# Decayed attention and two feed-forward layers on one core: the block quad's products in another order, low parts of sums on GpSimd, the high part of g and the low part of weights one step later

## The chip, the cores and the metric

One core of one Trainium2 chip. The kernel is one launch; the metric is the device time of that launch in microseconds (us), the median of repeated runs. All numbers are float32 at the interface.

## The reference

The reference computes a causal attention with decay and puts its output through two feed-forward layers:

```python
# attention, per batch (2) and head (8), 768 positions in blocks, head size 64
intra = ((q_b @ k_b.T) * Dmask) @ v_b            # Dmask[i, j] = lam ** (i - j), i >= j
inter = (q_b * lam ** (pos + 1)) @ kv_state
out_b = intra + inter
kv_state = lam ** block * kv_state + (k_b * lam ** (block - 1 - pos)).T @ v_b
...
x = out.reshape(1536, 512)                       # 1536 tokens, 512 features
h = x @ w_in1;  g = h * clip(h + 3, 0, 6) / 6;  x = g @ w_out1     # d_ff = 2048
h = x @ w_in2;  g = maximum(h, 0) ** 2;         out = g @ w_out2
```

The weights of the layers arrive as float64, the rest as float32.

## The kernel before

**Split numbers.** TensorE multiplies in a float32 format of fewer bits (F32R). Every operand is therefore held as a high part (the number rounded to F32R, made by a cast on ScalarE) and a low part (the number less its high part, made on VectorE), and a product is three matmuls: high by high, high by low, low by high. A matmul here has a 128x128 stationary operand and a 128x512 moving one.

**Weights.** A tile of weights (512 KB of float64) is loaded by SyncE into one of three raw buffers and decoded by ScalarE and VectorE in five pieces, `decode_steps` (L155): `shift` (ScalarE L168 and VectorE L169; it also asks ScalarE for the magnitude of the next tile, L149), `join` (VectorE L174, and the cast to the high part, ScalarE L177), `clamp` of the next tile (L153), `add` (VectorE L181), `rest` (VectorE L184: the low part). A decoded tile takes a slot: five for input weights (`wi`), six for output weights (`wo`). There are 16 `wi` and 16 `wo` tiles to a layer, 64 in all.

**Layers.** The 1536 tokens are three blocks j = 0, 1, 2 of 512. The 2048 hidden features are 16 tiles f, in groups g of four. For each group the hidden products h are made, g is computed from them in `gate` (L450: for the first layer ScalarE L457, VectorE L459, ScalarE cast L463, VectorE low part L465; for the second ScalarE L461, L462, L463, VectorE L465), and `project` (L584) adds the group's contribution to the four output tiles of a block: `y(j, g)` is four units of 12 matmuls, each followed by an addition to `acc` on VectorE (L606) or, in the first group, a copy on ScalarE (L603).

**The quad.** In groups 1 to 3, blocks 0 and 1 by a pair of feature tiles (p = f // 2) form a 2x2 block product that `seven` (L498) makes of seven block products of six matmuls instead of eight, with sums of weights (`weight_sums`, GpSimd L204, four differences into `Ts`; split by `weight_sums_split` L214 into `Th` on ScalarE L222 and `Tl` on VectorE L224) and sums of tokens (`token_sums`, GpSimd L482; split in L494 and L496). `seven` is a generator: each `yield` ends a step. Its seven steps need, in the order of the code before: the first weight tile; `Th`, `Tl` number 3; number 2; the first tile's second half; number 1; number 4; the second tile. Copies between PSUM banks (ScalarE L529, L535, L539) and two additions (VectorE L545, L548) tie them together. `Th` and `Tl` have one buffer, so the next pair's split must follow the last use of this pair's.

**What sets the order.** All engines but SyncE run in the order of the code (`manual_schedule`). The units of TensorE's work stand in a hand-written list, `units` (L667): `q` is a step of a quad, `y` an output tile, `h` a block of hidden products outside the quads, `t` a `weight_sums_split`. Between them a planner with fixed costs (`UNIT` 2.72, `ONE` 0.44, `TWO` 0.7, `FOUR` 1.24, `SCALAR` 0.8) keeps two clocks, `pe_t` and `dve_t`: `vector` (L255) and `unit` (L260) call `decode_until` (L247), which puts decode pieces into VectorE's and ScalarE's queues as long as `dve_t` lies behind. `weight` (L266) forces the pieces of a tile that is needed and not decoded. A `wo` tile's slot comes free after the last unit of `y(2, g)`, which stands in group g + 1; of the four `wo` tiles of a group two fit into slots ahead and two, called the later ones below, must wait for that.

Of the kernel before, what the change touches and what calls it, by code (L numbers as in the profile page):

```python
# [17 lines left out]
P = 128  # L18
# [15 lines left out]
def decay_attention_moe_moe(  # L34
# [120 lines left out]
    def decode_steps(n):  # L155
# [16 lines left out]
        def join():  # L172

            nc.vector.scalar_tensor_tensor(  # L174
                u, t[:, :, 1], -(2**31), u, op0=ALU.bitwise_and, op1=ALU.bitwise_or
            )
            nc.scalar.copy(hi, u.bitcast(F32))  # L177

        def add():

            nc.vector.tensor_tensor(up, u, up, op=ALU.add)  # L181

# [6 lines left out]
        steps = [(ONE, shift), (TWO, join), (ONE, lambda: clamp(n + 1)), (TWO, add), (TWO, rest)]  # L189
        if kind == "wi" and f >= GROUP:  # L190
            full_t[layer, f] = up.bitcast(F32)
            if f % 2:
                steps.append((0.01, lambda: weight_sums(layer, f // 2)))
        return steps

# [15 lines left out]
    def sums_free():  # L211
        return not t_sum and keys[n_begun - 1][1] in s_done

    def weight_sums_split(layer, p):  # L214
# [8 lines left out]
        vector(dve_t + 2 * SCALAR, FOUR)  # L223
        nc.vector.tensor_tensor(lo, t, hi.bitcast(F32), op=ALU.subtract)  # L224
        t_t[layer, p] = (hi, lo)

    def decode_piece():
        nonlocal n_begun
        if not pieces:
            if n_begun == len(keys):  # L230
                return 0
            if not w_free[keys[n_begun][0]]:
                return 0
            pieces.extend(decode_steps(n_begun))
            n_begun += 1
# [46 lines left out]
    ident = const.tile([P, P], F32, name="ident")  # L282
# [77 lines left out]
    def state_values(c):  # L360
# [13 lines left out]
        if not last:  # L374
# [7 lines left out]
            else:  # L382
                kvs = ap.tile([P, NP, D], F32, tag="kvs", name="kvs", bufs=1)
# [66 lines left out]
    def gate(layer, j, f, ph):  # L450
# [34 lines left out]
    def token_sums_split(layer, n):  # L485
# [9 lines left out]
        vector(dve_t + 2 * SCALAR, FOUR)  # L495
        nc.vector.scalar_tensor_tensor(lo, t, scale, hi.bitcast(F32), op0=ALU.mult, op1=ALU.subtract)  # L496
# [5 lines left out]
    def seven(layer, p):  # L502
# [26 lines left out]
        nc.scalar.copy(b, a)  # L529
        yield  # L530
# [237 lines left out]
```

## Time and profile before

| | us |
|---|---|
| median of 3 runs (650.87 to 652.54) | 652.13 |
| the profiled execution | 651.67 |
| its span, first to last instruction | 649.9 |
| TensorE busy in it | 583.5 |
| VectorE busy | 414.5 |
| ScalarE busy | 327.4 |
| GpSimd busy | 96.4 |

"Busy" is the union of an engine's instruction times. Matmuls overlap each other, so that 90% busy is not 90% of the peak; what TensorE lost is read from how many matmuls lie in a stretch. "Idle before" of an instruction is the time in which its engine did nothing in front of it, with the instruction that ended the wait behind the arrow. PEclk is the clock that TensorE was granted: 1.00 is 2.4 GHz, 0.50 is 1.2 GHz.

### The profile page before, as it was taken

Reading aid. Unit: us, or ns where it says so; the run is one execution under the profiler, and the core shown is the slowest. Engines: PE = TensorE matmul, PEld = TensorE weight load, DVE = VectorE, ACT = ScalarE, POOL = GpSimd, SP = SyncE. Lnnn points to the kernel's source line nnn. Section 1 sums busy time; section 2 is a strip of 40 time slices with the busy share of each in tenths; the row PEclk is TensorE's granted clock in tenths of the full one; section 3 lists DMA queues with packets and bytes.
Section 4 is the critical chain, followed back from the end, with each engine's and each line's share of the span. In section 5 each row is a group of like instructions: output and inputs, shape, how many; then the busy total and the mean of one; then the engine's idle time right before and its main releaser. Section 6 shows DMA issues by size and latency. Waiting matters only on the chain. (4 is left out here: it accounts for less than half of the span.)

```text
span 649.9 us, 7777 instructions
## 1 busy us (share of the span) xinstructions
PE 583.5 (90%) x2950; PEld 464.2 (71%) x2950; DVE 414.5 (64%) x639; ACT 327.4 (50%) x545; POOL 96.4 (15%) x92
## 2 busy tenths in 40 slices
PE   8899989986999869988799989987899869989797
PEld 5677767865787648866588878776688648877586
DVE  6799986636974489555998763634982369433422
ACT  2344666545443365344654874758454485256120
POOL 3785102200210002100021012200210002100000
PEclk9899999999899979999799999999799979999699
DMA  9952220300420024000331210400420024000012
GB/s 327 406 212 89 72 98 32 98 0 27 136 98 0 2 86 140 32 1 0 130 98 33 88 42 0 131 0 7 155 97 1 1 74 153 1 0 1 32 66 97
DMA packets 18037, 49.79 MB, mean 77 GB/s; under 512 B 2128, under 2 KB 2128, under 8 KB 18000
## 3 DMA queue, kind: packets, MB, share of 16 engines
q1 hardware_dynamic: 17856, 49.04, 21.6%
q8 instruction: 23, 0.38, 0.2%
q10 hardware_dynamic: 144, 0.26, 0.2%
q14 instruction: 14, 0.11, 0.1%
HBM read 46.14 MB, written 3.15 MB: 76 GB/s over the span
## 5 line engine op out<-in xcount | busy, mean ns | idle before, releaser
L606 DVE TENSOR_TENSOR acc<-acc,py 128x512 f32<-128x512 f32 x72 | 49.1, 682 | 51.9 <-PE py L568 51.6
L441 PE MATMUL ph<-xh,wih 128*128 128x512 f32 x192 | 75.1, 391 | 3.1 <-DVE g L459 3.1
L441 PE MATMUL ph<-xh,wil 128*128 128x512 f32 x192 | 74.7, 389 | 0.0
L441 PE MATMUL ph<-xl,wih 128*128 128x512 f32 x192 | 74.7, 389 | 0.0
L204 POOL TENSOR_TENSOR Ts<-dt 128x256 f32<-128x256 f32 x24 | 20.8, 886 | 330.2 <-DVE dt L181 203.2
L181 DVE CUSTOM_DVE_ANT_0 dt<-da,dt 128x1024 uint16<-128x1024 uint16 x64 | 48.6, 759 | 0.1
L174 DVE SCALAR_TENSOR_TENSOR da<-raw,da 128x512 int32<-128x512 int32 x64 | 47.3, 739 | 1.7
L149 ACT ACTIVATE da<-raw 128x512 f32<-128x512 f32 x64 | 42.5, 664 | 3.8 <-DVE dt L181 3.4
L441 PEld LDWEIGHTS ph<-xh,wih 128*128 128x128 f32 x192 | 36.0, 188 | 11.5 <-DVE g L459 4.0
L168 ACT ACTIVATE dt<-raw 128x512 int32<-128x512 uint32 x64 | 42.9, 670 | 0.0
L441 PEld LDWEIGHTS ph<-xh,wil 128*128 128x128 f32 x192 | 36.0, 188 | 7.6
L441 PEld LDWEIGHTS ph<-xl,wih 128*128 128x128 f32 x192 | 36.0, 188 | 7.4
L153 DVE TENSOR_SCALAR da<-da 128x512 f32<-128x512 f32 x64 | 32.5, 509 | 13.3 <-ACT da L149 13.0
L568 PE MATMUL py<-woh,gA 128*128 128x512 f32 x80 | 32.0, 414 | 4.7 <-ACT woh L177 4.7
L169 DVE TENSOR_SCALAR da<-da 128x512 int32<-128x512 int32 x64 | 36.0, 562 | 0.0
L177 ACT CAST woh<-da 128x512 fp32r<-128x512 f32 x32 | 19.7, 616 | 29.3 <-DVE da L174 29.1
L459 DVE SCALAR_TENSOR_TENSOR g<-g,ph 128x512 f32<-128x512 f32 x24 | 16.4, 684 | 27.5 <-ACT g L457 27.5
L462 ACT ACTIVATE g<-g 128x512 f32<-128x512 f32 x48 | 30.4, 632 | 1.5
L517 PE MATMUL pq<-S,Th 128*128 128x512 f32 x96 | 29.9, 392 | 1.1 <-ACT pq L529 1.0
L177 ACT CAST wih<-da 128x512 fp32r<-128x512 f32 x32 | 19.8, 618 | 20.0 <-DVE da L174 19.8
L465 DVE TENSOR_TENSOR gA<-g,gA 128x512 fp32r<-128x512 f32 x19 | 13.3, 700 | 25.0 <-ACT gA L463 24.9
L457 ACT ACTIVATE g<-pq,three 128x512 f32<-128x512 f32 x24 | 16.4, 685 | 23.0 <-PE pq L517 23.0
(159 smaller groups left out, 1453.4 us busy)
## 6 DMA issues: line engine op xcount, KB each, us to landing
raw<-in_w_in SPq DMA_DIRECT2D x32, 512.0 KB, 3.2
raw<-in_w_out SPq DMA_DIRECT2D x32, 512.0 KB, 3.3
out<-acc SPq DMA_DIRECT2D x12, 256.0 KB, 2.0
kT<-in_kT SPq DMA_DIRECT2D x6, 256.0 KB, 5.5
k<-in_k SPq DMA_DIRECT2D x6, 256.0 KB, 5.6
v<-in_v SPq DMA_DIRECT2D x6, 256.0 KB, 5.0
lentS<-in_kT SPq DMA_DIRECT2D x6, 256.0 KB, 5.2
lentS<-in_qT SPq DMA_DIRECT2D x6, 256.0 KB, 5.4
```

Of the source, the lines that this page charges most:

```text
L149: nc.scalar.activation(abs_t[n], raw_t[n][:, :, 1].bitcast(F32), AF.Abs, scale=2.0**16)
L153: nc.vector.tensor_scalar(abs_t[n], abs_t[n], 2.0, (1.875 - 2.0**-23) * 2.0**32, op0=ALU.max, op1=ALU.min)
L168: nc.scalar.activation(up, t[:, :, 0].bitcast(U32), AF.Copy, scale=2.0**-29)
L169: nc.vector.tensor_scalar(u, u, 3, None, op0=ALU.logical_shift_left)
L174: nc.vector.scalar_tensor_tensor(u, t[:, :, 1], -(2**31), u, op0=ALU.bitwise_and, op1=ALU.bitwise_or)
L177: nc.scalar.copy(hi, u.bitcast(F32))
L181: nc.vector.tensor_tensor(up, u, up, op=ALU.add)
L441: nc.tensor.matmul(ph, w[:, a * P : (a + 1) * P], x[:, a, :], start=a == 0 and i == 0, stop=a == KD - 1 and i == 2,)
L462: nc.scalar.activation(g, g, AF.Square)
L517: nc.tensor.matmul(ps, u, v, start=start and a == 0 and i == 0, stop=a == KH - 1 and i == 2, skip_group_check=True)
L568: nc.tensor.matmul(py, a, b, start=f == fs[0] and i == 0, stop=f == fs[-1] and i == 2)
L606: nc.vector.tensor_tensor(t, t, py, op=ALU.add)
```

## The change

It reorders the steps of a quad (the first tile's second half becomes step 2) and the units of groups 1 to 3 (the four units of `y(2, g - 1)` come earlier); it makes the high part of a decoded weight in `add`, from the joined number as before, and its low part in the next tile's pieces; in the first layer it makes the high and low part of g at the next call of `settle`; it takes the products with the low part of g last in an output tile; it moves the low parts of weight sums, and of the first layer's token sums, from VectorE to GpSimd; and it gives a third buffer to g, paid for by letting `ident` and `kvs` share the buffers `Th` and `Ts`.

```diff
         def join():
...
-            nc.scalar.copy(hi, u.bitcast(F32))
-
         def add():
             nc.vector.tensor_tensor(up, u, up, op=ALU.add)
+            nc.scalar.copy(hi, u.bitcast(F32))
+            rests.append((TWO, rest))
+            if kind == "wi" and f >= GROUP and f % 2:
+                rests.append((0.01, lambda: weight_sums(layer, f // 2)))
...
-        steps = [(ONE, shift), (TWO, join), (ONE, lambda: clamp(n + 1)), (TWO, add), (TWO, rest)]
         if kind == "wi" and f >= GROUP:
             full_t[layer, f] = up.bitcast(F32)
-            if f % 2:
-                steps.append((0.01, lambda: weight_sums(layer, f // 2)))
+        steps = [(ONE, shift), (TWO, join), (ONE, lambda: clamp(n + 1)), (TWO, add)]
+        steps[1:1] = rests
+        rests.clear()
         return steps
...
     def sums_free():
-        return not t_sum and keys[n_begun - 1][1] in s_done
+        return not t_sum and min(full_t)[0] in s_done
...
         nc.scalar.copy(hi, t)
-        vector(dve_t + 2 * SCALAR, FOUR)
-        nc.vector.tensor_tensor(lo, t, hi.bitcast(F32), op=ALU.subtract)
+        nc.gpsimd.tensor_tensor(lo, t, hi.bitcast(F32), op=ALU.subtract)
...
-    ident = const.tile([P, P], F32, name="ident")
+    ident = wsp.tile([P, 2 * DM], F32, tag="Th", name="ident")[:, :P]
...
-                kvs = ap.tile([P, NP, D], F32, tag="kvs", name="kvs", bufs=1)
+                kvs = wsp.tile([P, KD, DM // 2], F32, tag="Ts", name="kvs")[:, :, :D]
...
-        g = gp.tile([P, n], F32, tag="g", name="g")
+        g = gp.tile([P, n], F32, tag="g", name="g", bufs=3)
+        g_t[layer, j, f] = (gh, gl, s)
         if layer == 0:
             nc.scalar.activation(g, ph, AF.Relu, bias=three)
             vector(pe_t + SCALAR, TWO)
             nc.vector.scalar_tensor_tensor(g, g, 6.0, ph, op0=ALU.min, op1=ALU.mult)
+            settle()
+            unsplit.append((g, gh, gl))
         else:
             nc.scalar.activation(g, ph, AF.Relu)
             nc.scalar.activation(g, g, AF.Square)
-        nc.scalar.copy(gh, g)
-        vector(dve_t + SCALAR if layer == 0 else pe_t + 3 * SCALAR, TWO)
-        nc.vector.tensor_tensor(gl, g, gh.bitcast(F32), op=ALU.subtract)
-        g_t[layer, j, f] = (gh, gl, s)
+            unsplit.append((g, gh, gl))
+            settle(pe_t + 2 * SCALAR)
+
+    def settle(ready=0.0):
+        for g, gh, gl in unsplit:
+            nc.scalar.copy(gh, g)
+            vector(max(dve_t, ready) + SCALAR, TWO)
+            nc.vector.tensor_tensor(gl, g, gh.bitcast(F32), op=ALU.subtract)
+        unsplit.clear()
...
-        vector(dve_t + 2 * SCALAR, FOUR)
-        nc.vector.scalar_tensor_tensor(lo, t, scale, hi.bitcast(F32), op0=ALU.mult, op1=ALU.subtract)
+        if layer == 0:
+            nc.gpsimd.tensor_tensor(lo, t, hi.bitcast(F32), op=ALU.subtract)
+        else:
+            vector(dve_t + 2 * SCALAR, FOUR)
+            nc.vector.scalar_tensor_tensor(lo, t, scale, hi.bitcast(F32), op0=ALU.mult, op1=ALU.subtract)
...
         nc.scalar.copy(b, a)
+        settle()
+        yield
+        prod(a, wi(f0, 1), x(0, k2), False)
+        gate(layer, 0, f0, a)
         yield
...
         nc.scalar.copy(s7, e)
+        settle()
         yield
         prod(b, tw(2), s(2), False)
         c = bank()
         nc.scalar.copy(c, b)
+        vector(pe_t + SCALAR, TWO)
+        nc.vector.tensor_tensor(b, b, s7, op=ALU.add)
         yield
-        prod(a, wi(f0, 1), x(0, k2), False)
-        gate(layer, 0, f0, a)
-        yield
-        vector(dve_t, TWO)
-        nc.vector.tensor_tensor(b, b, s7, op=ALU.add)
         prod(c, tw(1), s(1), False)
...
-    def products(layer, j, grp, e, f, py):
+    def products(layer, j, grp, e, f, py, part=range(3)):
...
+        prods = ((woh, gh), (wol, gh), (woh, gl))
+        for i in part:
...
-            for f in fs:
-                products(layer, j, grp, e, f, py)
+            for part in ((0, 1), (2,)):
+                for f in fs:
+                    products(layer, j, grp, e, f, py, part)
...
-            units += q(p) * 3 + y2[:1] + q(p) * 2 + y2[1:2] + q(p) * 2 + [("t", l, p + 1)] + y2[2:3]
+            units += q(p) + y2[:1] + q(p) * 3 + y2[1:2] + q(p) * 2 + [("t", l, p + 1)] + y2[2:3] + q(p)
             p += 1
-            units += q(p) * 3 + h(2, f0) + q(p) * 2 + y2[3:] + q(p) * 2 + h(2, f1)
+            units += q(p) + y2[3:] + q(p) * 3 + h(2, f0) + q(p) * 2 + h(2, f1) + q(p)
             units += y(l, 1, g) + h(2, f2) + h(2, f3)
```

`settle()` is also called at the start of `project` and `project_by_unit`, and `decode_piece` emits waiting `rests` when no tile can be begun.

The first place where this shows is VectorE's queue in the second layer's group 2, from the addition of the last unit of `y(2, 1)` (L606 before, L628 now, into `acc_3363` and `acc_3341`) to the first of the two later `wo` tiles. Before:

```order
L606 TENSOR_TENSOR acc_3363<-acc_3363,py 128x512
L465 TENSOR_TENSOR gA<-g,gA 128x512 x2
L465 TENSOR_TENSOR gq<-g,gv 128x512
L169 TENSOR_SCALAR da<-da 128x512
L174 SCALAR_TENSOR_TENSOR da<-raw,da 128x512
L153 TENSOR_SCALAR da<-da 128x512
L181 ISA dt<-da,dt 128x1024
L184 TENSOR_TENSOR wol_924<-dt,woh_923 128x512
```

Now (L565 and L569 are the quad's additions L545 and L548, L481 is the low part of g, L180 and L187 are L181 and L184):

```order
L628 TENSOR_TENSOR acc_3341<-acc_3341,py 128x512
L481 TENSOR_TENSOR gq<-g,gv 128x512
L565 TENSOR_TENSOR pq<-pq,s_3982 128x512
L169 TENSOR_SCALAR da<-da 128x512
L174 SCALAR_TENSOR_TENSOR da<-raw,da 128x512
L153 TENSOR_SCALAR da<-da 128x512
L180 ISA dt<-da,dt 128x1024
L169 TENSOR_SCALAR da<-da 128x512
L187 TENSOR_TENSOR wol_899<-dt,woh_898 128x512
L174 SCALAR_TENSOR_TENSOR da<-raw,da 128x512
L481 TENSOR_TENSOR gdecay<-g,gdecay 128x512
L569 TENSOR_TENSOR pq_3975<-pq,s_3982 128x512
```

The decoding of the later tiles stood behind all gates of the second pair's steps and its addition L548; now it stands behind step 4's addition L565 and ahead of L569, and the low part L187 has the next tile's shift in front of it.

The second place is ScalarE's queue in the first layer's group 2, at the last gates before `y(1, 2)` and the casts of the two later `wo` tiles. Before:

```order
L457 ACTIVATE g<-pq,three 128x512
L463 CAST gkv<-g 128x512
L457 ACTIVATE g<-ph,three 128x512
L463 CAST gh_805<-g 128x512
L168 ACTIVATE dt<-raw 128x512
L149 ACTIVATE da<-raw 128x512
L177 CAST woh_1183<-da 128x512
L168 ACTIVATE dt<-raw 128x512
L149 ACTIVATE da<-raw 128x512
L177 CAST woh_1201<-da 128x512
```

Now (L464 is L457, L479 is L463, L181 is L177; `pq_1950` holds the second tile of block 1):

```order
L464 ACTIVATE g<-pq,three 128x512
L479 CAST gv<-g 128x512
L181 CAST woh_1190<-da 128x512
L464 ACTIVATE g<-pq_1950,three 128x512
L479 CAST gdecay<-g 128x512
L168 ACTIVATE dt<-raw 128x512
L149 ACTIVATE da<-raw 128x512
L464 ACTIVATE g<-ph,three 128x512
L479 CAST gh_834<-g 128x512
L464 ACTIVATE g<-pq,three 128x512
L479 CAST gkv<-g 128x512
```

Before, each gate's cast followed its own activation and both later tiles came behind the last gate. Now a cast follows the next gate's activation, and the tiles' pieces stand between the gates: the cast into `gh_834`, of the value in `pq_1950`, has a cast of the previous value, two pieces of a weight and another gate's activation in front of it.

The third place is GpSimd's queue at the start of the first layer's quads. Before:

```order
L482 TENSOR_TENSOR s_779<-xf_197,s_777 128x1024
L482 TENSOR_TENSOR s_940<-xf_197,xf_435 128x1024
L204 TENSOR_TENSOR Ts<-dt 128x256 x2
L204 TENSOR_TENSOR Ts<-dt,Ts 128x256 x2
L204 TENSOR_TENSOR Ts<-dt 128x256 x2
```

Now (L498 is L482, L512 the low part of token sums, L209 is L204, L228 the low part of weight sums):

```order
L498 TENSOR_TENSOR s_779<-xf_197,s_777 128x1024
L512 TENSOR_TENSOR S_930<-s_775,S_930 128x1024
L498 TENSOR_TENSOR s_933<-xf_197,xf_434 128x1024
L512 TENSOR_TENSOR S_1009<-s_777,S_1009 128x1024
L512 TENSOR_TENSOR S_1101<-s_779,S_1101 128x1024
L512 TENSOR_TENSOR xl_424<-s_933,xh_423 128x1024
L209 TENSOR_TENSOR Ts<-dt 128x256 x2
L209 TENSOR_TENSOR Ts<-dt,Ts 128x256 x2
L228 TENSOR_TENSOR Tl<-Ts,Th 128x1024
L209 TENSOR_TENSOR Ts<-dt 128x256 x2
```

Four low parts of token sums have joined it ahead of the first weight sums, and one low part follows each set of weight sums.

## Rows read from the trace of the kernel before

**Rows 1.** The page: busy time, and TensorE's granted clock in 40 slices.
```profile
PE 583.5 (90%) x2950; PEld 464.2 (71%) x2950; DVE 414.5 (64%) x639; ACT 327.4 (50%) x545; POOL 96.4 (15%) x92
...
PEclk9899999999899979999799999999799979999699
```

**Rows 2.** Waits of TensorE: engine, line, releaser, us in total, times, longest.
```profile
PE py L568 <- ACT woh L177: 29.3, 12, 4.3
PE pq L517 <- ACT Th L222: 8.4, 6, 1.7
PE py L568 <- DVE wol L184: 5.0, 9, 1.0
PE pq L517 <- DVE Tl L224: 3.2, 6, 0.5
```

**Rows 3.** The chain in order of time, a stretch without waits: start, us, what.
```profile
549.70 10.88 PE py L568 x48
```

**Rows 4.** Stretches round waits at y(1, g): us, PE busy, PEclk, DMA, GB/s.
```profile
155.00:170.00 15.00, 9.15 (x26) 0.77 0.33 105
449.00:464.00 15.00, 9.15 (x27) 0.77 0.31 106
598.00:613.50 15.50, 10.24 (x27) 0.67 0.04 17
```

**Rows 5.** The same view round waits for Th and Tl.
```profile
136.00:141.00 5.00, 2.92 (x11) 1.00 0.00 0
579.00:583.00 4.00, 2.34 (x9) 1.00 0.00 0
```

**Rows 6.** Timeline of ScalarE, first layer, group 2: start, us, instruction.
```profile
232.44 0.68 ACT L457 ACTIVATE g<-ph,three 128x512 f32<-128x512 f32 x1
233.89 0.62 ACT L463 CAST gh<-g 128x512 fp32r<-128x512 f32 x1 [0.77 <-DVE g L459]
234.41 0.67 ACT L168 ACTIVATE dt<-raw 128x512 int32<-128x512 uint32 x1
234.98 0.65 ACT L149 ACTIVATE da<-raw 128x512 f32<-128x512 f32 x1
235.54 0.60 ACT L177 CAST woh<-da 128x512 fp32r<-128x512 f32 x1
236.05 0.66 ACT L168 ACTIVATE dt<-raw 128x512 int32<-128x512 uint32 x1
```

**Rows 7.** The same view of VectorE, the later tiles' decoding.
```profile
237.41 0.42 DVE L169 TENSOR_SCALAR da<-da 128x512 int32<-128x512 int32 x1
237.86 0.69 DVE L174 SCALAR_TENSOR_TENSOR da<-raw,da 128x512 int32<-128x512 int32 x1
238.47 0.42 DVE L153 TENSOR_SCALAR da<-da 128x512 f32<-128x512 f32 x1
238.81 0.68 DVE L181 CUSTOM_DVE_ANT_0 dt<-da,dt 128x1024 uint16<-128x1024 uint16 x1
239.60 0.69 DVE L184 TENSOR_TENSOR wol<-dt,woh 128x512 fp32r<-128x512 f32 x1
240.21 0.42 DVE L169 TENSOR_SCALAR da<-da 128x512 int32<-128x512 int32 x1
```

**Rows 8.** Groups of instructions by line: VectorE's low parts of sums, ScalarE's Th.
```profile
L224 DVE TENSOR_TENSOR Tl<-Ts,Th 128x1024 fp32r<-128x1024 f32 x12 | 14.7, 1222 | 1.5 <-ACT Th L222 1.5
...
L222 ACT CAST Th<-Ts 128x1024 fp32r<-128x1024 f32 x12 | 12.5, 1046 | 4.7 <-POOL Ts L204 4.7
```

**Rows 9.** Timeline of GpSimd and VectorE at one token sum.
```profile
345.66 2.71 POOL L482 TENSOR_TENSOR s<-acc,s 128x1024 f32<-128x1024 f32 x1 [4.04 <-DVE acc L606]
346.03 2.62 DVE L153 TENSOR_SCALAR da<-da 128x512 f32<-128x512 f32 x1
...
348.57 0.68 DVE L614 SCALAR_TENSOR_TENSOR xl<-acc,xh 128x512 fp32r<-128x512 f32 x1
```

**Rows 10.** Timeline of TensorE: the first hidden product, and waits in the first groups.
```profile
55.65 0.50 PE L441 MATMUL ph<-xh,wih 128*128 128x512 f32 x1
...
78.92 0.50 PE L441 MATMUL ph<-xh,wih 128*128 128x512 f32 x1 [1.22 <-DVE g L459]
...
83.84 0.50 PE L441 MATMUL ph<-xh,wih 128*128 128x512 f32 x1 [1.90 <-DVE g L459]
...
383.97 0.50 PE L568 MATMUL py<-woh,gv 128*128 128x512 f32 x1 [1.69 <-ACT gv L463]
...
645.73 0.39 PE L568 MATMUL py<-woh,gkv 128*128 128x512 f32 x1
```

More of the change, by code (lines that the diff above doesn't have):

```diff
@@ L187, in rest @@
             load_ahead(n + 1 + RAW)
-        steps = [(ONE, shift), (TWO, join), (ONE, lambda: clamp(n + 1)), (TWO, add), (TWO, rest)]
         if kind == "wi" and f >= GROUP:
             full_t[layer, f] = up.bitcast(F32)
-            if f % 2:
-                steps.append((0.01, lambda: weight_sums(layer, f // 2)))
+        steps = [(ONE, shift), (TWO, join), (ONE, lambda: clamp(n + 1)), (TWO, add)]
+        steps[1:1] = rests
+        rests.clear()
         return steps
+    rests = []
     full_t, t_sum, t_t, s_done = {}, {}, {}, set()
@@ L229, in decode_piece @@
         if not pieces:
[L230 to L235, printed above, removed]
+            if n_begun < len(keys) and w_free[keys[n_begun][0]]:
+                pieces.extend(decode_steps(n_begun))
+                n_begun += 1
+            else:
+                pieces.extend(rests)
+                rests.clear()
+        if not pieces:
+            return 0
         if pieces[0][0] < ONE and not sums_free():
@@ L462, in gate @@
             nc.scalar.activation(g, g, AF.Square)
-        nc.scalar.copy(gh, g)
-        vector(dve_t + SCALAR if layer == 0 else pe_t + 3 * SCALAR, TWO)
-        nc.vector.tensor_tensor(gl, g, gh.bitcast(F32), op=ALU.subtract)
-        g_t[layer, j, f] = (gh, gl, s)
+            unsplit.append((g, gh, gl))
+            settle(pe_t + 2 * SCALAR)
+    unsplit = []
+    def settle(ready=0.0):
[4 more added lines that the diff above has]
+        unsplit.clear()
     s_sum, s_t = {}, {}
@@ L494, in token_sums_split @@
         nc.scalar.activation(hi, t, AF.Copy, scale=scale)
-        vector(dve_t + 2 * SCALAR, FOUR)
-        nc.vector.scalar_tensor_tensor(lo, t, scale, hi.bitcast(F32), op0=ALU.mult, op1=ALU.subtract)
+        if layer == 0:
+            nc.gpsimd.tensor_tensor(lo, t, hi.bitcast(F32), op=ALU.subtract)
+        else:
+            vector(dve_t + 2 * SCALAR, FOUR)
+            nc.vector.scalar_tensor_tensor(lo, t, scale, hi.bitcast(F32), op0=ALU.mult, op1=ALU.subtract)
         if n == 1:
@@ L556, in seven @@
         gate(layer, 0, f1, c)
-    def products(layer, j, grp, e, f, py):
+    def products(layer, j, grp, e, f, py, part=range(3)):
         es = slice(e * P, (e + 1) * P)
-        fs = range(GROUP * grp, GROUP * (grp + 1))
         gh, gl, _ = g_t[layer, j, f]
         woh, wol = weight(("wo", layer, f))
-        if layer == 0:
-            prods = ((woh[:, es], gh), (woh[:, es], gl), (wol[:, es], gh))
-        else:
-            prods = ((gh[:, es], woh), (gh[:, es], wol), (gl[:, es], woh))
-        for i, (a, b) in enumerate(prods):
-            nc.tensor.matmul(py, a, b, start=f == fs[0] and i == 0, stop=f == fs[-1] and i == 2)
+        prods = ((woh, gh), (wol, gh), (woh, gl))
+        for i in part:
+            w, g = prods[i]
+            a, b = (w[:, es], g) if layer == 0 else (g[:, es], w)
+            nc.tensor.matmul(py, a, b, start=f % GROUP == 0 and i == 0, stop=f % GROUP == GROUP - 1 and i == 2)
     def project_by_unit(layer, j, grp, f):
         n = BLOCKS[j] * P
+        settle()
         free_weights()
@@ L588, in project @@
         fs = range(GROUP * grp, GROUP * (grp + 1))
+        settle()
         if py is None:
```

## The prediction

> **What bounds the kernel now.** I read the page first: TensorE is busy 90% of the span, VectorE 64%, ScalarE 50%, GpSimd 15%, and TensorE's granted clock dips to 0.7 and below at regular distances [rows 1]. So TensorE is the bound, and the dips ask what it waits for.
>
> The chain's stretches without waits give the price of its work: 48 matmuls in 10.88 us, 0.2267 us each [rows 3]. By the code the layers have 576 (L441), 504 (L517) and 1152 (L568) of them: 2232, or 506.0 us. The first starts at 55.65 and the last ends at 646.12 [rows 10], 590.5 us. TensorE thus loses 84.5 us, in idle time and at the lower clock.
>
> The waits name the places [rows 2]: y(1, g) waits for the two later `wo` tiles (29.3 + 5.0 us), quads for `Th` and `Tl` (8.4 + 3.2). What such a place costs in all, clock included, is read from stretches around it. A matmul is shown for 0.39 us but follows its neighbour at 0.2267, so at the edges 1.7 more are counted than fit, and the loss is length - (count - 1.7) x 0.2267. At y(1, g) that is 9.5, 9.3 and 9.8 us [rows 4]; there are six such places (groups 1 to 3, two layers): **57 us**. The clock of these stretches is 0.77 to 0.67: after the waits TensorE runs matmuls at 1.2 GHz for some us. Round `Th` and `Tl` it is 2.9 in the first layer and 2.4 in the second, at a clock of 1.00 [rows 5]; six places, 11.6 us by the waits alone, 15.9 by these two: **15 us**. The other 12 us lie in the layers' first groups and at small waits.
>
> **The change, part by part.**
>
> *Order of units.* Before, 2 steps and one h stand between the end of y(2, g - 1), which frees the slots, and y(1, g): 2 x 1.36 + 2.72 = 5.4 us. Now 6 steps and two h do: 13.6 us. The decoding begins in VectorE's queue behind step 4's addition L565, 1.4 us into the last 9.5 us of those. I walk ScalarE's and VectorE's queues from the end of step 4 (t = 0), with the distances from start to start that the timelines show [rows 6, 7] (ScalarE 0.52 to 0.57, and 0.65 where one needs the other; VectorE 0.60, 0.34 for L153, 0.45 for L169, 0.80 from L181 to L184). y(1, g) starts at 9.5, and its first two tiles take four matmuls (0.9 us) now that the low parts of g come last.
>
> First layer: first later tile decoded at 5.7, second at 11.0; needed at 10.4 and 11.1. So the weights are in time, by little. The value in `pq_1950` is not: its activation is behind the cast of a weight that waits for L180 at 7.9, and its cast stands behind two weight pieces and the activation of h(2, f1) (the second order shown above); it ends at 11.8, wanted at 10.9: 0.9 us. Its low part is ready at 13.7, wanted at 13.0: 0.8 us. A wait costs about 0.3 more than its idle time (at `Th` and `Tl` 15 for 11.6 in twelve waits), so two of them make **2.2 us** a group, 6.6 for three.
>
> Second layer: three ScalarE instructions to a gate but only one of VectorE. The tiles are ready at 6.0 and 10.5, the high part of the fourth tile's g at 11.3, wanted at 10.9: **0.7 us** a group, 2.1 for three.
>
> *What the walk hides.* Eight tiles a group are now decoded between step 4 and the group's end, about 37 us: 8 x 2.8 us (from one L169 to the next [rows 7]) + 9 additions and 14 gate pieces of 0.6 = 36 us of VectorE in the first layer. It just fits. Should it not, what is late next is L628's additions, which hold PSUM banks; three banks give 5 us of slack, so I take nothing.
>
> *Th and Tl.* They now have 9.5 us of TensorE's work (y, step 7, step 1, y, step 2) between the end of step 6 and their first use, where they had 4.1. ScalarE needs two gates and 1.05 for `Th` [rows 8], about 5 in all; `Tl` on GpSimd is not in the trace, but the nearest row, a token sum of the same shape and engine, has 2.71 [rows 9]. Lowest bound 1.22, VectorE's own [rows 8]; highest 2.71 plus one VectorE instruction of 0.7 in front. I take 2.7: 5 + 2.7 = 7.7 < 9.5. All **15 us** go, with 2 us to spare.
>
> *Low parts on GpSimd.* Sixteen instructions of 1.22 leave VectorE. In return each can hold it: L153 took 2.62 instead of 0.42 while a token sum ran, and ended 0.3 us after it [rows 9]. At worst that is 16 x (2.6 - 1.2) = 22 us of VectorE, at best a gain of 20. In the quads VectorE has nothing but gate parts with TensorE's slack before them; I take nothing there.
>
> The Trainium skill (GPSIMD Engine Reference, Engine selection) says to leave elementwise work on VectorE, GpSimd being about twice as slow. The rows agree on the size (2.71 against 1.22), and by that rule alone this part would be a loss: with all 22 us on TensorE's path the sum below would be 610.
>
> *First groups.* In the first layer the late cast takes a wait out of ScalarE's chain (0.77 us a gate [rows 6]), but three GpSimd instructions hold VectorE among the gates, and a fourth delays the first `Ts`, for which a decode activation then waits in ScalarE's queue ahead of four output copies. I walk it to 3 us lost before y(0, 0) and 3 at y(1, 0), where 6.2 were lost: nothing gained. In the second layer gh of the last tile stays late (1.69 before [rows 10]; I get 2.5), and the small waits behind it go: -1.5.
>
> *At no cost:* the third g buffer, the shared `ident` and `kvs` (each is dead before the next user writes; attention's GpSimd chain is as long), `rest` one piece later (0.45 us, with `wi` tiles decoded 10 us ahead). Loads move with `rest`: SyncE asks for a raw tile 0.45 us later, against three buffers.
>
> **The sum,** against the profiled execution: 651.7 - 57 - 15 + 6.6 + 2.1 - 1.5 = 586.9; I add 1 for waits of a few tenths that no walk finds: 588. The median of the runs is 0.5 above the profiled one, so **588.3**.
>
> **The rivals.**
>
> 1. *The walk is short at y(1, g).* If VectorE comes one hold (2.6 us) late there, TensorE waits about 5 us instead of 2.2, and the clock falls as it does now. Price: a stretch loses 9.5 [rows 4], of which 5.7 is idle ((29.3 + 5.0) / 6 [rows 2]), so the clock and restarts take 3.8; (2.6 + 3.8) x 6 = 38, **626**. For it: the first layer's margins are tenths. Against it: `Tl` is over 4 us before y(2, g - 1) ends, so no hold lies in that stretch, and the waits of about 2 us for `Th` and `Tl` leave the clock at 1.00 [rows 5].
>
> 2. *Slower: GpSimd's hold sets VectorE's pace.* Each of sixteen low parts would hold a gate long enough that TensorE waits 2.6 us and loses 3.8 at the lower clock: 16 x 6.4 = 102, 588 + 102 = **690**. It decides from the point at which TensorE's slack behind the held instruction is under 2.6 us. Against it: in the quads that slack is a whole y (2.72) or more at every gate, and the hold of [rows 9] falls into a slice (the 22nd) whose clock is 0.9 or more [rows 1]. The rule of the Trainium skill named above (GPSIMD Engine Reference, Engine selection) points this way.
>
> 3. *The change does not do what it says.* The planner's clocks put the later tiles' pieces so far back that y(1, g) forces them as before; then only `Th` and `Tl` go: **637**. The order shows them ahead, so this needs a wait at run time that the queue's order does not show, as for a slot or a raw tile.
>
> 4. *Better:* no wait at y(1, g) at all and half of the first groups' losses gone: 652.1 - 72 - 5 = **575** to 580.
>
> **How the numbers follow.** Forecast 0.68 (580 to 600), better 0.10, rival 1 0.12, rival 3 0.05, rival 2 0.03, no change 0.02. The range takes in the better case's nearer half, 577; above, a wait of one hold at each y(1, g) without the clock's fall, 588 + 16 = 604, and the 2 us of `Tl`'s spare: 606. Left out are rivals 1 to 3, 2 in 10. About 0.3% (2 us) is what a measurement can tell: faster 0.95, within it 0.02, slower 0.03.
>
> **What would show it.** Right: the waits for L181 (the cast of `wo`) and for `Th` are gone from TensorE's list; what stands there is L479's cast, one to two us a place, three in the first layer larger than three in the second; PEclk is 1.00 in the middle of every group; `Tl` L228 on GpSimd takes 2.4 to 2.9; VectorE instructions of over 2 us beside it. Wrong: PEclk still dips once a group (rival 1), TensorE waits on VectorE right behind L228 (rival 2), or L181 leads the list (rival 3).

## The result, and the profile after

| | us | ratio to the kernel before, 95% interval |
|---|---|---|
| before, in the same session | 651.64 | |
| changed kernel | 578.32 (577.75 to 579.11) | 0.8875 [0.8857, 0.8893] |
| forecast | 588.3 (577 to 606) | |
| profiled execution | 577.75, span 576.0 | |

The kernel is 73 us faster, 10 us more than forecast. The time is inside the range, 1.3 us above its lower end; it lies among the times of rival 4 (575 to 580), which had a chance of 0.10, and not among the forecast's own (580 to 600). The page of the changed kernel, the lines that answer to [rows 1]:

```profile
PE 555.6 (96%) x2950; PEld 456.8 (79%) x2950; DVE 407.8 (71%) x623; ACT 323.4 (56%) x545; POOL 143.4 (25%) x108
...
PEclk9999999999999999999999999999999999999999
```

The same 2950 matmuls are busy for 28 us less, because in the layers they no longer run at a lower clock: every slice of PEclk is 0.9 or more, where each group had one of 0.8, 0.7 or 0.6. GpSimd has 47 us more. The waits of TensorE (engine, line, releaser, us in total, times, longest), all of 0.5 us or more:

```profile
PE psc L361 <- DVE A L362: 6.4, 6, 2.5
PE py L587 <- ACT gh L479: 2.1, 1, 2.1
PE py L587 <- ACT acc L625: 1.7, 1, 1.7
PE warm L661 <- DVE idle L295: 1.5, 1, 1.5
PE py L587 <- DVE gkv L481: 1.3, 2, 0.7
PE pq L536 <- ACT pq L548: 0.9, 1, 0.9
PE pxt L402 <- DVE A L362: 0.8, 1, 0.8
PE py L587 <- DVE gq L481: 0.7, 1, 0.7
PE py L587 <- DVE gl L481: 0.7, 1, 0.7
```

All four waits of [rows 2] are gone: TensorE has no wait in this list for the casts of `wo` (now L181), for its low parts (L187), for `Th` (L227) or `Tl` (L228). psc, warm and pxt belong to the attention ahead of the layers, which the change leaves alone but for the shared buffers. Two stretches round y(1, 1), first and second layer, as in [rows 4]:

```profile
147.00:162.00 15.00, 14.27 (x63) 1.00 0.30 102
402.00:417.00 15.00, 15.00 (x68) 1.00 0.31 106
```

63 matmuls stand where 26 stood, at a clock of 1.00. By the prediction's formula the first loses 15 - 61.3 x 0.2267 = 1.1 us and the second nothing, where 9.5 and 9.3 were lost. And the two ends of the layers:

```profile
56.10 0.50 PE L447 MATMUL ph<-xh,wih 128*128 128x512 f32 x1
...
571.80 0.39 PE L587 MATMUL py<-woh,gA 128*128 128x512 f32 x1
```

The layers take 516.1 us for 506.0 us of matmuls. TensorE loses **10 us** there, where it lost 84.5; the difference, 74 us, is that of the two spans (649.9 and 576.0).

### The profile page after: what moved, and what is told of

Its sections match the earlier page's. It is cut to its first block, busy times and chain, and to the rows that moved or that the text cites. A ratio compares the mean times of both kernels' runs of the same rounds, so it can differ in the third digit from the quotient of the medians.

```text
span 576.0 us, 7778 instructions
## 1 busy us (share of the span) xinstructions
PE 555.6 (96%) x2950; PEld 456.8 (79%) x2950; DVE 407.8 (71%) x623; ACT 323.4 (56%) x545; POOL 143.4 (25%) x108
## 4 chain that ended last, share of the span: by engine, by line
PE 73%; DVE 13%; ACT 5%; issue 4%; DMA 2%; SPq 1%; POOL 1%; DVEq 0%
PE py L587 39%; PE pq L536 19%; PE ph L447 14%; DVE dt L180 2%; DVE da L153 1%; DVE da L174 1%; DVE g L466 1%; DMA lentS<-in_qT 1%; DVE xl L419 1%; DVE A L362 1%; DMA lentS<-in_k 1%; DVE wol L187 1%; ACT da L149 1%; DVE da L169 1%; POOL Ts L209 1%
## 5 line engine op out<-in xcount | busy, mean ns | idle before, releaser
L628 DVE TENSOR_TENSOR acc<-acc,py 128x512 f32<-128x512 f32 x72 | 48.7, 683 | 34.6 <-PE py L587 34.5
L209 POOL TENSOR_TENSOR Ts<-dt 128x256 f32<-128x256 f32 x24 | 22.6, 963 | 160.7 <-DVE dt L180 136.6
L228 POOL TENSOR_TENSOR Tl<-Ts,Th 128x1024 fp32r<-128x1024 f32 x12 | 29.9, 2492 | 103.3 <-ACT Th L227 81.9
L180 DVE CUSTOM_DVE_ANT_0 dt<-da,dt 128x1024 uint16<-128x1024 uint16 x64 | 50.7, 792 | 0.0
L174 DVE SCALAR_TENSOR_TENSOR da<-raw,da 128x512 int32<-128x512 int32 x64 | 48.0, 750 | 0.3
L153 DVE TENSOR_SCALAR da<-da 128x512 f32<-128x512 f32 x64 | 35.5, 555 | 2.9 <-ACT da L149 2.9
L169 DVE TENSOR_SCALAR da<-da 128x512 int32<-128x512 int32 x64 | 36.8, 575 | 0.0
L481 DVE TENSOR_TENSOR gq<-g,gv 128x512 fp32r<-128x512 f32 x20 | 16.0, 801 | 25.6 <-ACT gv L479 25.5
L181 ACT CAST wih<-da 128x512 fp32r<-128x512 f32 x32 | 19.9, 620 | 19.3 <-DVE da L174 19.3
L464 ACT ACTIVATE g<-pq,three 128x512 f32<-128x512 f32 x24 | 16.2, 690 | 25.4 <-PE pq L536 24.9
L587 PE MATMUL py<-woh,gA 128*128 128x512 f32 x80 | 29.8, 389 | 0.0
L187 DVE TENSOR_TENSOR wol<-dt,woh 128x512 fp32r<-128x512 f32 x32 | 23.8, 742 | 7.5 <-ACT woh L181 7.5
```

What stands on the lines that cost most here:

```text
L153: nc.vector.tensor_scalar(abs_t[n], abs_t[n], 2.0, (1.875 - 2.0**-23) * 2.0**32, op0=ALU.max, op1=ALU.min)
L169: nc.vector.tensor_scalar(u, u, 3, None, op0=ALU.logical_shift_left)
L174: nc.vector.scalar_tensor_tensor(u, t[:, :, 1], -(2**31), u, op0=ALU.bitwise_and, op1=ALU.bitwise_or)
L228: nc.gpsimd.tensor_tensor(lo, t, hi.bitcast(F32), op=ALU.subtract)
L587: nc.tensor.matmul(py, a, b, start=f % GROUP == 0 and i == 0, stop=f % GROUP == GROUP - 1 and i == 2)
L628: nc.vector.tensor_tensor(t, t, py, op=ALU.add)
```

## The experiments

Theory A is the prediction's: the order of steps and units makes the gain. Theory B: the relief of VectorE and ScalarE (low parts on GpSimd, later casts, low parts of g last) makes it, and the order only goes with it. Theory C, within A: a good part of the price was the clock that fell behind the idle time. "Loss" below is start-to-start time of TensorE beyond 0.2267 us a matmul, "late" a wait of TensorE for the thing named. Unless another base is named, an edit is made to the changed kernel.

**The order alone.** The kernel before with the new order of steps and units:

```diff
         nc.scalar.copy(b, a)
         yield
+        prod(a, wi(f0, 1), x(0, k2), False)
+        gate(layer, 0, f0, a)
+        yield
...
-            units += q(p) * 3 + y2[:1] + q(p) * 2 + y2[1:2] + q(p) * 2 + [("t", l, p + 1)] + y2[2:3]
+            units += q(p) + y2[:1] + q(p) * 3 + y2[1:2] + q(p) * 2 + [("t", l, p + 1)] + y2[2:3] + q(p)
             p += 1
-            units += q(p) * 3 + h(2, f0) + q(p) * 2 + y2[3:] + q(p) * 2 + h(2, f1)
+            units += q(p) + y2[3:] + q(p) * 3 + h(2, f0) + q(p) * 2 + h(2, f1) + q(p)
```

> The kernel before with the new order of the quad's seven steps and of the units alone; every cast, low part and sum stays where it was before. Theory A (the order makes the gain): the wo slots come free 13.6 us of TensorE's work ahead of y(1, g) instead of 5.4, and t stands 9.5 us ahead of its use instead of 4.1, so nearly all of 57 + 15 us goes; a low part or a high part of g that is a few tenths to 2 us late stays at each of the six y(1, g): 582 to 598 us, L181 and L222 gone from TensorE's waits. Theory B (the relief of VectorE and ScalarE makes the gain, the order only goes with it): the tiles still come late, 610 us or more, the granted clock still dips once a group. Theory C (much of the price was the clock that follows the idle time, 3.8 of 9.5 us a place): as A, and the granted clock is 0.99 or more although waits of 1 to 2 us stay.

Measured: 588.61 us, ratio 0.9027 [0.9004, 0.905]. Of the gain of 73 us, 63 come from the order alone; theory B's 610 or more is out. Waits of TensorE for the steps and the layers:

```profile
PE ph L441 <- DVE g L459: 3.1, 2, 1.9
PE py L568 <- ACT gh L463: 3.0, 2, 2.8
...
PE py L568 <- DVE wol L184: 1.4, 2, 0.7
```

L177 (29.3 us before) and L222 (8.4) are gone from the list. The first line is that of the first group, unchanged from before [rows 10]; the third shows that two tiles are still late, by 0.7 us each.

**All but the order.** The changed kernel with the two `units` lines and the steps of the quad as they were.

> The changed kernel with the old order of the quad's steps and of the units; low parts on GpSimd, the later high part of g, the later low part of the weights and the products with the low part of g at the end stay. Theory A: 5.4 us of TensorE's work between the free slots and y(1, g) cannot hide two decodings, the 57 us stay but for a few us, and Tl on GpSimd (2.5 us instead of 1.22) makes the waits at Th and Tl longer, 15 to 25 us: 640 to 662 us, the clock dips once a group. Theory B: the relief shortens the decoding enough, 595 to 620 us.

Measured: 644.84 us, ratio 0.9881 [0.9861, 0.9901]. Theory A, within its range. Its waits:

```profile
PE py L587 <- ACT woh L181: 22.6, 12, 4.1
PE py L587 <- DVE wol L187: 10.4, 12, 1.7
PE pq L536 <- POOL Tl L228: 7.5, 6, 1.7
...
PE pq L536 <- ACT Th L227: 3.4, 3, 1.1
```

At y(1, g) TensorE is idle for 33.0 us, against 34.3 before: the relief only moves the wait from the cast to the low part. `Tl` on GpSimd, used 4.1 us after t stands, is waited for longer than on VectorE (7.5 against 3.2 in [rows 2]), but `Th`, which is waited for first, for less (3.4 against 8.4); the two together take 10.9 us against 11.6. By layers they differ: a place costs 0.8 us of idle time in the first, where it cost 2.2, and 2.8 in the second, where it cost 1.7. Whether the move of `Tl` alone is a loss in the old order is not shown, as no run makes it without the other edits.

**The low parts back on VectorE.**

```diff
-        nc.gpsimd.tensor_tensor(lo, t, hi.bitcast(F32), op=ALU.subtract)
+        vector(dve_t + 2 * SCALAR, FOUR)
+        nc.vector.tensor_tensor(lo, t, hi.bitcast(F32), op=ALU.subtract)
         t_t[layer, p] = (hi, lo)
```

and, for the first layer's tokens, the line on VectorE of the kernel before.

> The changed kernel with the low parts of the sums (twelve Tl, four of tokens) back on VectorE. Theory A: VectorE gets 16 x 1.22 = 20 us of work back and loses the holds beside GpSimd; in the quads it has slack either way: 576 to 582 us, within 1% of the changed kernel. Theory B: the relief is needed, VectorE's queue is full over the group (36 us of 37), so 1.22 us a quad comes on top of waits at y(1, g) and the PSUM banks: 12 x 1.22 = 15 us more, 588 to 600.

Measured: 580.31 us, ratio 0.8895 [0.8879, 0.8911]. The interval overlaps with that of the changed kernel: GpSimd is worth 2 us by the medians, which is within the noise, and 3.5 at most by the ends of the intervals. The trace shows both sides of it: at two of the first layer's y(1, g) the high part of g is now late by 0.85 us and a weight by 0.32, while in the first layer's first group the wait for `acc` L625 is gone. And 1.6 us of the profiled difference come from the clock behind a wait that is as long as before (the last section).

**g split at once in the first layer.** `settle()` behind `unsplit.append` instead of ahead of it.

> The changed kernel with the first layer's high and low part of g right behind the gate, not one step later. Theory A: the cast stands in ScalarE's queue waiting for VectorE's product, some 0.6 us a gate, which matters only at the three y(1, g) of the first layer and its first group, where the low part is 0.7 us late already: 0 to 2 us each, 578 to 585. Theory B: ScalarE's queue and with it the decoding's casts come late at every gate, 590 or more.

Measured: 579.09 us, ratio 0.8883 [0.8867, 0.8899]: no difference that can be told. The three waits of 0.7 us at y(1, g) are gone, as expected; a wait of 1.1 us for L466 has come in the first group, and that for L479 in the second layer is 3.1 us.

**The weights' parts as they were** (cast in `join`, low part in the tile's own pieces).

```diff
-        steps = [(ONE, shift), (TWO, join), (ONE, lambda: clamp(n + 1)), (TWO, add)]
-        steps[1:1] = rests
+        steps = [(ONE, shift), (TWO, join), (ONE, lambda: clamp(n + 1)), (TWO, add), (TWO, rest)]
```

> The changed kernel with a weight's high part cast again from its first join, and its low part again in its own tile's pieces, not one tile later. Theory A (the order makes the gain): two instructions change places within a queue that has its slack; the cast of the second later wo tile stands a few tenths of a us elsewhere: 576 to 582 us. Theory B (the later parts are what fits the decoding into the group): the waits for L187 and for the cast come back at y(1, g), 0.5 to 2 us at each of six places with the clock behind them, 585 to 600.

Measured: 583.12 us, ratio 0.8936 [0.8919, 0.8953], between the two ranges: this part is worth 4.8 us by the medians and 4.0 by the ratios, the most of the four parts beside the order. No weight is late, so theory B's reason is wrong; what comes back is small waits in the first groups, and one for g at each y(1, g) of the first layer, here y(1, 2) in TensorE's timeline:

```profile
218.15 0.50 PE L584 MATMUL py<-gh,woh 128*128 128x512 f32 x1 [0.85 <-ACT gh L476]
...
219.91 0.49 PE L584 MATMUL py<-gl,woh 128*128 128x512 f32 x1 [0.33 <-DVE gl L478]
```

This is the wait that the prediction expected of the changed kernel (0.9 us for the high part, then the low part).

**Products in the old order,** tile by tile.

> The changed kernel with the products of each tile in the old order (high with high, high of the weight with low of g, low of the weight with high of g, tile by tile). Theory A: the first two tiles then take six matmuls before the third is wanted instead of four, which gives the weights 0.45 us more, and takes from the last tile's low part of g some 0.25 us: the three waits of 0.7 us for it in the first layer become about 1 us, 578 to 582 us in all. Theory B (the low parts last are needed): the low part of g is wanted 1.5 us earlier and every y(1, g) waits 2 us and more with the clock behind it, 590 to 610.

Measured: 579.31 us, ratio 0.8881 [0.8868, 0.8894]: theory A. The three waits for the low part are 0.97 us instead of 0.72, as worked out; no difference in the whole that can be told.

**The slots free later, twice.** The place of `y2[3:]` in the second quad (the texts on record call it two outputs; it is the fourth one alone):

```diff
-            units += q(p) + y2[3:] + q(p) * 3 + h(2, f0) + q(p) * 2 + h(2, f1) + q(p)
+            units += q(p) * 4 + y2[3:] + h(2, f0) + q(p) * 2 + h(2, f1) + q(p)      # 9.5 us ahead
+            units += q(p) * 4 + h(2, f0) + y2[3:] + q(p) * 2 + h(2, f1) + q(p)      # 6.8 us ahead
```

> The changed kernel with y2's last two outputs, which free the wo slots, behind the fourth step of the second quad instead of the first: 9.5 us of TensorE's work between them and y(1, g) instead of 13.6. Theory A in the form of the prediction: the decoding starts behind step 4's addition on VectorE in either case, 9.5 us ahead of y(1, g), so the extra 4.1 us do nothing: 576 to 582 us. Theory A in the plain form (every us that the slots come free earlier is used): 4.1 us less of margin, the second tile 2 us late, waits of 2 us or more at six places, 592 to 610.

> The changed kernel with y2's last two outputs behind the first h of the second quad: 6.8 us of TensorE's work between the free slots and y(1, g), against 5.4 before the change and 13.6 after. Theory A: two decodings of 2.8 us and more, with the gates of VectorE between them, take about 9 us from L565, so the second tile is 2 to 4 us late, and the clock falls with it as it did before: 5 to 9 us at each of six places, 608 to 632 us, the clock dips once a group. Theory B: with VectorE and ScalarE relieved, 6.8 us are nearly enough: under 595. The price of a wait by its length is read from this run and the others: in the runs so far one of 2.1 us left the clock at 1.00 and one of 2.8 us did not.

Measured at 9.5 us: 590.6 us, ratio 0.9061 [0.9041, 0.908]. The time is close to the plain form's, the trace is not: no wait for L181 or L187 is in its list, so the tiles are in time, as the prediction's form says. Most of the loss is elsewhere:

```profile
PE pq L536 <- ACT pq L548: 8.3, 7, 2.1
```

`y2[3:]` stood between steps 1 and 2 of the quad, and step 2 writes on in the bank that L548 copies first. With the output gone from there nothing hides that copy. With the clock behind one of them, these waits lose 10.6 of the 14.3 us by which the layers lose more than in the changed kernel. The rest is mostly at the first layer's y(1, g), where the low part of g is late by 1.3 to 1.6 us instead of 0.7 (2.3 us more), and behind the second layer's wait for L479 (1.6 us more, the last section). The unit had two uses, and neither theory had seen the second.

Measured at 6.8 us: 635.76 us, ratio 0.9748 [0.973, 0.9766], theory A, 4 us beyond its upper end:

```profile
PE py L587 <- ACT woh L181: 21.3, 12, 4.1
PE py L587 <- DVE wol L187: 9.6, 12, 1.4
```

The waits for L548 are there too (8.3 us). From 6.8 to 9.5 us of distance the time falls by 45 us. The run without the order, at 5.4 us, is 9 us slower than that at 6.8, but not at y(1, g): its six places lose 53.3 us, here 53.1. It differs by the waits for `Th` and `Tl`, 14.8 us of loss, which the order of the steps takes away, less what L548 costs here.

So 1.4 us more of distance bought nothing and the next 2.7 nearly all. The code of the kernels has the reason, which the prediction and the texts above pass over: a slot is given back not with the last unit that reads it but at the next call of `free_weights`, which stands at the start of an h, of a y and of a quad's first step. Behind `y2[3:]` that is the next h. It is h(2, f1) in the kernel before, 2.7 us of TensorE's work ahead of y(1, g), and in the run at 6.8, 4.1 us ahead; it is h(2, f0) in the changed kernel and in the run at 9.5, 9.5 us ahead in both. VectorE's first piece of the first later tile, first layer, group 2, in the run at 9.5 and in that at 6.8:

```profile
206.36 0.42 DVE L169 TENSOR_SCALAR da<-da 128x512 int32<-128x512 int32 x1
...
222.74 0.42 DVE L169 TENSOR_SCALAR da<-da 128x512 int32<-128x512 int32 x1
```

It starts 8.7 us ahead of y(1, 2) (at 215.1) in the first and 1.2 us ahead (of 223.9) in the second; in the changed kernel 8.1 us ahead, in the kernel before 3.5 us behind its start. A version that gives the slots back right behind `y2[3:]` was not run.

**GpSimd's hold doubled.**

```diff
         nc.gpsimd.tensor_tensor(lo, t, hi.bitcast(F32), op=ALU.subtract)
+        nc.gpsimd.tensor_tensor(t, t, hi.bitcast(F32), op=ALU.subtract)
```

> The changed kernel with a second, useless GpSimd subtraction of the same size right behind each of the twelve Tl (into t, which is dead then): the hold of VectorE is doubled. Theory A (VectorE has slack where it is held): nothing beyond a few tenths at the gates: 578 to 583 us. Rival 2 of the prediction (GpSimd's hold sets VectorE's pace): 12 more holds of about 2.5 us that reach TensorE, with the clock behind some of them, 2.6 to 6.4 us each, 610 us or more. In between, 583 to 600, the second hold of a pair is where VectorE's slack ends.

Measured: 584.04 us, ratio 0.8954 [0.8934, 0.8974], the case in between. In the profiled execution the layers lose 6.7 us more (the medians differ by 5.7), all of it at two places behind a held VectorE instruction: 1.7 us at the first quad's L549, and the larger one, in the second layer, from the timelines of GpSimd, VectorE, ScalarE and TensorE:

```profile
372.87 2.71 POOL L229 TENSOR_TENSOR Ts<-Ts,Th 128x1024 f32<-128x1024 f32 x1
...
373.26 2.88 DVE L174 SCALAR_TENSOR_TENSOR da<-raw,da 128x512 int32<-128x512 int32 x1
...
376.17 0.62 ACT L181 CAST woh<-da 128x512 fp32r<-128x512 f32 x1 [3.26 <-DVE da L174]
...
380.77 0.62 ACT L549 COPY pq<-pq 128x512 f32<-128x512 f32 x1
...
381.44 0.80 PE L537 MATMUL pq<-xh,wih 128*128 128x512 f32 x1 [3.17 <-ACT pq L549]
```

GpSimd's useless subtraction holds L174 for 2.88 instead of 0.68 us, a cast behind it waits 3.26, the copy behind that comes late, and TensorE waits 3.17 instead of 0.94 us; with the lower clock behind it (0.72 from 377 to 389) the place loses 6.2 instead of 1.2 us. So rival 2's mechanism exists, at 2 of 12 places, with a hold twice as long.

**What is left, taken away.** Two versions, for the waits still in the list. The first takes three edits: in groups 1 to 3 of the first layer g is split at once; the tokens' low parts are back on VectorE; the split of S2 moves behind the first output of y(1, 0).

> The changed kernel with three edits for the waits that its trace still shows: in the first layer's groups 1 to 3 the high and low part of g come right behind the gate (the three waits of 0.7 us at y(1, g)); the tokens' low parts of the first layer are back on VectorE (the wait of 1.7 us at the first group's y(1, 0) for a copy behind them); in the second layer the split of S2 moves behind the first output of y(1, 0) (1.0 of the 2.1 us for the high part of g there). If the waits are what is left of the loss, 3 x 1.0 + 1.0 to 2.0 + 1.0 go, 5 to 6 us: 572 to 575 us. If each only passes its time to the next wait in ScalarE's or VectorE's queue: 577 to 580.

Measured: 575.13 us, ratio 0.881 [0.8792, 0.8828]. The first two edits took their waits away; the third did not: two activations of the decoding moved up into the place of S2, and TensorE waits 2.2 us as before. The second version keeps the two and takes another third edit:

```diff
             unsplit.append((g, gh, gl))
+            if f >= GROUP:
+                settle()
...
-        if layer == 0:
-            nc.gpsimd.tensor_tensor(lo, t, hi.bitcast(F32), op=ALU.subtract)
...
-        units += h(2, f0) + s(1) + h(2, f1) + h(1, f2) + h(0, f2) + s(2) + h(1, f3) + h(0, f3)
+        units += h(2, f0) + s(1) + h(2, f1) + h(1, f2)
+        units += h(0, f2) + s(2) + h(1, f3) + h(0, f3) if l == 0 else h(1, f3) + h(0, f2) + s(2) + h(0, f3)
```

> As best_first, but the split of S2 back at its place, and in the second layer's first group h(1, f3) ahead of h(0, f2), so that the gate y(1, 0) waits for is 2.7 us further ahead of it on ScalarE. In best_first the wait of 2.2 us there stayed after S2 had left, because two activations and a cast of the decoding moved up into its place. If the place of the gate in ScalarE's queue is what counts: the wait goes and 2 us with it, 572 to 574 us. If the decoding moves up again, or the high part of the weights of h(1, f3) is late one h earlier: 575 to 578 us.

Measured: **571.61 us**, ratio 0.8759 [0.8737, 0.878], the fastest of all, 6.7 us below the changed kernel. Of TensorE's waits in the layers one is left:

```profile
PE psc L361 <- DVE A L362: 6.9, 6, 3.0
PE warm L660 <- DVE idle L295: 1.5, 1, 1.5
PE pq L535 <- ACT pq L547: 0.9, 1, 0.9
PE pxt L402 <- DVE A L362: 0.8, 1, 0.8
```

The layers now lose 3.5 us; what is left to win lies in the attention.

## Why the prediction was right, and 10 us too high

**y(1, g), 57 us, and Th and Tl, 15 us: right.** Both are gone, and the runs with and without the order show that it is the order that takes them. The run at 6.8 us tells its two halves apart: the place of the units takes the 57, the order of the steps with the place of t the 15. The walk started where the decoding starts, behind L565; the 5.4 and 13.6 us that the prediction set ahead of it are not its cover, since the slots come back 2.7 and 9.5 us ahead. Once its inputs are there, `Tl` takes 2.49 us on GpSimd (29.9 over twelve), where 2.7 were taken. In the first layer's second group L228 ends at 196.5 us, and step 3 first reads `Tl` at 200.8, 4.3 us later, where 2 were expected.

**New waits at y(1, g), 6.6 + 2.1 us: mis-sized.** They are 3 x 1.0 and 0. This is the step of the sum that was furthest out, by 5.7 us, and the timelines of the changed kernel show by how little it went wrong. Step 4 ends where h(2, f0) starts, at 203.04, which is t = 0. TensorE, VectorE and ScalarE, first layer, group 2:

```profile
203.04 0.39 PE L447 MATMUL ph<-xh,wih 128*128 128x512 f32 x1
...
212.56 0.39 PE L587 MATMUL py<-gv,woh 128*128 128x512 f32 x1
...
213.93 0.40 PE L587 MATMUL py<-gh,woh 128*128 128x512 f32 x1
...
215.96 0.50 PE L587 MATMUL py<-gl,woh 128*128 128x512 f32 x1 [0.72 <-DVE gl L481]
...
203.84 0.70 DVE L565 TENSOR_TENSOR pq<-pq,s 128x512 f32<-128x512 f32 x1
...
207.98 0.68 DVE L187 TENSOR_TENSOR wol<-dt,woh 128x512 fp32r<-128x512 f32 x1
...
212.48 0.69 DVE L187 TENSOR_TENSOR wol<-dt,woh 128x512 fp32r<-128x512 f32 x1
...
215.22 0.69 DVE L481 TENSOR_TENSOR gl<-g,gh 128x512 fp32r<-128x512 f32 x1
...
213.09 0.64 ACT L479 CAST gh<-g 128x512 fp32r<-128x512 f32 x1
```

| us after step 4 | walk | measured |
|---|---|---|
| y(1, g) starts | 9.5 | 9.5 |
| first later tile decoded | 5.7 | 5.6 |
| second | 11.0 | 10.1 |
| high part of the last g, and when it is wanted | 11.8, 10.9 | 10.7, 10.9 |
| its low part | 13.7 | 12.9 |

The walk is right at the first tile and 0.8 to 1.1 us late at all that follows. The high part is then ready 0.2 us before it is wanted instead of 0.9 after, the low part is late by 0.7, and two waits at 2.2 us become one at 1.0. In the second layer the same high part is ready at 409.85 and used at 410.10, 0.2 us ahead too (walk: 0.4 late). Margins of tenths at the end of a walk of 10 us were taken as if the walk were good to tenths. The two runs that put VectorE's work back (low parts of sums, weights' low parts) bring the wait of 0.85 us for the high part back, at two and at three of the first layer's three places, so the queue that the walk described is the right one. Of the signs that the prediction named one did not come: at y(1, g) TensorE waits for the low part, L481, in the first layer alone, and not for L479's cast.

**First groups, 6 us to stay in the first layer: 2.8.** The wait for `acc` behind the first `Ts` is there with 1.7 us (2.0 lost; forecast 3), and it goes where the tokens' low parts return to VectorE, as it should by the reason given. The 3 us ahead of y(0, 0) are 0.8, although VectorE is held there (an L481 of 2.91 us at 83.4). In the second layer 3.6 are lost, 2.9 were forecast (the wait for the high part is 2.1 us, 2.5 by the walk, and a copy is late by 0.9). "1 us for waits that no walk finds", on top of what stood elsewhere, wasn't needed.

Together: 5.7 at y(1, g), about 3 in the first group and 2 of small waits less than forecast, 0.7 more in the second layer: 10 us.

These errors nearly all have one sign. That the time is inside the range all the same is owed to the range's lower end, which had been taken down into rival 4's times.

**The rivals.** Rival 1 (walk short) erred on the wrong side. Rival 3's mechanism (637) is what the run at 6.8 us makes: the waits at y(1, g) are back, those for `Th` and `Tl` are not, and it takes 635.76. Rival 4's time is what came, though not all of its reason: three waits at y(1, g) are left, of 1.0 us of loss each. Rival 2's hold is in the trace, without its price; GpSimd's and VectorE's timelines, first layer:

```profile
130.49 2.40 POOL L228 TENSOR_TENSOR Tl<-Ts,Th 128x1024 fp32r<-128x1024 f32 x1 [10.55 <-ACT Th L227]
...
171.44 2.62 POOL L228 TENSOR_TENSOR Tl<-Ts,Th 128x1024 fp32r<-128x1024 f32 x1 [4.81 <-ACT Th L227]
...
130.97 2.47 DVE L481 TENSOR_TENSOR gl<-g,gh 128x512 fp32r<-128x512 f32 x1 [0.77 <-ACT gh L479]
...
171.72 1.28 DVE L628 TENSOR_TENSOR acc<-acc,py 128x512 f32<-128x512 f32 x2
172.91 1.44 DVE L169 TENSOR_SCALAR da<-da 128x512 int32<-128x512 int32 x1
```

L481, which takes 0.69 us alone, takes 2.47 and ends 0.55 us after L228; beside seven of the twelve L228 a VectorE instruction shows 2.0 us or more. Behind six of the seven TensorE shows no wait that leads back to them. From the seventh, at 369.40, a cast that waits for VectorE leads to the copy L548 and its 0.9 us; that is the place that the doubled hold made worse. The Trainium skill (GPSIMD Engine Reference, Engine selection) would have left these subtractions on VectorE. The durations agree (2.49 against 1.22). The run with them back on VectorE says that in this order the choice makes no difference clear of the noise; what it makes in the old order is not shown by itself.

## What to carry to other kernels

Where the bound engine waits for a buffer that comes free late, look at the order of its own work first: moving units that are needed anyway ahead of the wait gave 63 of 73 us here, and four ways of relieving the other engines gave 7 by themselves. Measure the distance from where the code gives the buffer back, which here is not where it is last read. Price such a wait from the whole stretch round it, clock included, not from the idle time: 34 us of idle time lost 57. And a unit that is moved leaves a place behind; ask what it was hiding there.

## What the runs showed of the hardware that was not expected

**The same wait, another clock.** Idle time of TensorE of equal length may or may not lower its clock. First the changed kernel, round its wait of 2.10 us for L479 at 346.1:

```profile
344.00:352.00 8.00, 5.90 (x27) 1.00 0.01 3
```

then the run with the slots free 9.5 us ahead, round the same wait (2.08 us) and round one of 2.10 us for L548:

```profile
349.00:357.00 8.00, 5.92 (x19) 0.79 0.01 4
399.00:408.00 9.00, 6.90 (x24) 0.81 0.00 0
```

The first loses 2.4 us, the others 4.0 each, with matmuls 0.43 us apart (1.2 GHz) behind the wait, where they are 0.23 apart at 2.4. The run with the low parts back on VectorE lost 4.0 behind the same wait, too (2.09 us, clock 0.79). The wait for the same cast in the run with the weights' parts as they were is longer, 2.51 us, and leaves the clock alone, with a loss of 2.8:

```profile
349.00:357.00 8.00, 5.78 (x25) 1.00 0.01 2
```

Waits of 2.8 to 3.2 us lowered it in each of three runs (losses of 4.8 to 6.2 us). So did three short ones of 0.2, 0.4 and 0.7 us close together, at y(1, 2) of the run with the order alone:

```profile
218.00:228.00 10.00, 8.66 (x29) 0.83 0.32 104
```

There they lose 3.8 us; the same three at y(1, 3) of that run (0.2, 0.4 and 0.7 us) lose 2.2 and leave the clock at 1.00.
That 2.1 us leaves the clock alone, as an expectation above reads from the runs until then, thus doesn't hold in general; what decides between waits of one length stays open. Theory C holds in this form: in the layers of the changed kernel, with single waits of 0.5 to 2.1 us, the clock stayed at 1.00, and of the 57 us at y(1, g) before 23 were more than idle time, by the estimate from the stretches.

**Who holds whom.** Beside L228 the additions to `acc`, which read one operand from PSUM, ran at 0.64 us each (1.28 for two at 171.72), as without it, and the next instruction, L169 with one operand in SBUF, was held from 172.91 to the end of L228. The Trainium skill (SBUF — State Buffer, Who interferes with whom) says that a VectorE instruction contends with GpSimd's reads when both its inputs are in SBUF, and with GpSimd when it runs in a two-port mode; L481 and L628 agree with the first, and L169 fits the second, though no run here shows its mode. At one place GpSimd was the one to wait: a token's low part shows 5.00 us in place of 2.4, GpSimd's timeline and VectorE's last instruction of a row without gaps:

```profile
92.48 5.00 POOL L512 TENSOR_TENSOR S<-s,S 128x1024 fp32r<-128x1024 f32 x1 [6.71 <-ACT S L510]
...
94.53 0.68 DVE L187 TENSOR_TENSOR wil<-dt,wih 128x512 fp32r<-128x512 f32 x1
```

VectorE ran six instructions back to back over it until 95.2; from there 2.3 us are left, the length of such an instruction alone. Spans on GpSimd are rough, so this is one reading of one place.
